# Attention in residue-class order, with 512-token MLP groups interleaved with the next batch's attention

## The chip, the cores and the metric

One core of one Trainium2 chip. The metric is the device time of one execution in microseconds (us); each kernel has three or four executions in rounds shared with the kernel before. Engines: PE is TensorE, PEld its weight loads, DVE VectorE, ACT ScalarE, POOL GpSimd, SP the queue that stores the output. In the kernels, PSUM tiles take what TensorE writes (matmul results and transposes) and SBUF tiles hold everything else; AV is the product of the attention weights with v. The granted clock is the share of its full clock that TensorE was given, as the profile records it.

## The reference, cut to what matters

```python
# q, k, v: (8 batches, 8 heads, 576 tokens, 64), drawn at 0.1 * randn
rel = pos[:, None] - pos[None, :]
mask_plain = (rel >= 0) & (rel < 32)                              # heads 0..3
mask_dil = (rel >= 0) & (rel < 32 * 4) & (rel % 4 == 0)           # heads 4..7
attn = softmax(where(mask, q @ k.T / 8, -1e9)) @ v
x = attn.transpose(0, 2, 1, 3).reshape(4608, 512)
h = x @ w_in                                                       # 512 -> 2048
out = (h * sigmoid(h)) @ w_out                                     # 2048 -> 512
```

Dilated heads look at every fourth token. If tokens are sorted by residue modulo 4 (their class), a dilated head becomes a dense band of 32 within each class of 144 tokens.

## The kernel before

Per batch: transposes of q and k, then five steps over 128-token blocks with scores, exp, mask, AV, and between them the second MLP layer of the batch before; then the whole first MLP layer with nothing beside it.

```python
for nat_t, tT in ((k_nat, kT), (q_nat, qT)):          # 40 transposes, 8 copies of 128x576
    for hp in range(HP):
        tps = ps.tile([P, NC * P], F16, tag="ps", ...)
        for c in range(NC): nc.tensor.transpose(tps[...], nat_t[:ns, c, 2*hp : 2*hp+2, :], ident[...])
        nc.vector.tensor_copy(tT[:, hp, :], tps[:, :S])
# ... cut
for step in range(NC + 2):
    for h in range(H):                                 # scores: keys of a block x 256 queries
        nc.tensor.matmul(sp[:nkv, :nq], kT[...], qT[...], start=True, stop=True)
        nc.scalar.activation(pt[:nkv, :nq], sp[:nkv, :nq], AF.Exp, scale=scale)
        meng = nc.vector if h < 4 else nc.gpsimd       # mask
        meng.tensor_tensor(pt[:nkv, :nq], pt[:nkv, :nq], masks[...], ALU.mult)
    if b > 0 and step < NC: moe_l2(b - 1, step)        # 16 matmuls of 512 columns
    # ... cut: AV, normalisation, transposes back into xT
for f in range(NFF):                                   # first layer: 384 + 192 columns
    for (w0, wn) in L1W:
        for mc in range(4): nc.tensor.matmul(hps[:, :wn], w_in16[...], xT[:, mc, w0:w0+wn], ...)
        nc.scalar.activation(sig[:, :wn], hps[:, :wn], AF.Sigmoid)
        nc.vector.tensor_tensor(gt[:, w0:w0+wn], hps[:, :wn], sig[:, :wn], ALU.mult)
```

The softmax here doesn't subtract the row's maximum and nothing guards it: scores larger than these inputs give would overflow.

## Time and profile before

| | before |
|---|---|
| time | 453.8 us (452.43 to 455.7, 3 runs); 454.27 with the run beside the changed kernel |
| first MLP matmul | 54.3 us |
| period of a batch | 51.1 us: 32.1 attention and second layer, 19.0 first layer |

The page of the kernel before: busy time of each engine, then its PE and PE clock rows (40 equal slices of the span, in tenths), then the chain of waits by engine.

```profile
PE 405.1 (89%) x3041; PEld 240.8 (53%) x3041; DVE 269.2 (59%) x851; ACT 194.2 (43%) x592; POOL 195.0 (43%) x294
...
PE   2670599899999999999999999999999999999996
...
PEclk9999999898999989998999989998999989998999
...
PE 74%; DVE 10%; DMA 5%; POOL 5%; ACT 3%; issue 1%; ACTq 0%; POOLq 0%
```

PE is busy nearly throughout and the chain runs through it, but a busy matmul unit need not be doing much. The windows view divides one period (and looks once more at the first 3.7 us of its first-layer part). Columns: stretch and length, busy us of each engine with the number of instructions, granted TensorE clock, DMA share, GB/s.

```profile
178.70:210.80 32.10, 30.43 (x235) 16.09 (x235) 19.63 (x67) 10.41 (x41) 20.59 (x31) 1.00 0.69 75
210.80:229.80 19.00, 19.00 (x149) 13.54 (x148) 14.28 (x41) 13.83 (x34) 3.45 (x5) 0.91 0.49 33
210.70:214.40 3.70, 3.70 (x19) 2.37 (x18) 1.28 (x9) 2.26 (x4) 3.55 (x5) 0.54 1.11 73
```

The third line is the one to see: at the start of the first layer the clock is about half. The timeline shows what came just before. Columns: start, duration, engine, line, operation, tiles, rows*columns of the weights, output.

```profile
206.88 0.19 PE L195 MATMUL av_3_1_2979<-v_3_1971,p_2_7_2733 128*128 128x65 f16 x1
206.91 0.19 PE L195 MATMUL av_3_1_2979<-v_3_1971,p_3_7_2848 128*128 128x65 f16 x1
...
207.26 0.22 PE L195 MATMUL av_4_0_3003<-v_3_1971,p_3_0_2813 128*64 128x65 f16 x1
207.41 0.21 PE L195 MATMUL av_4_0_3003<-v_3_1971,p_4_0_2909 64*64 64x65 f16 x1
```

AV matmuls with weights of equal size start 0.03 us apart; where the weights alternate between 128 and 64 rows (the last, short block) they start 0.15 us apart. These weights also have fewer columns, but the transposes of q show the same 0.15 us with 128 columns throughout: 0.06 us apart among four of 128 rows, 0.15 us to the one of 64 rows (178.98 to 179.13 us) and again back. The costliest groups of the page add the ScalarE table loads and the wait of the opening: the last column is the idle time before the group and what ended it.

```profile
L241 ACT ACT_TABLE_LOAD x8 | 10.3, 1283 | 61.6 <-PE h_0_0_1406 L233 9.0
L195 PE MATMUL av_3_1_510<-v_0_110,p_3_4_404 128*128 128x65 f16 x1 | 0.2, 233 | 16.9 <-POOL p_3_4_404 L179 16.9
...
L177 ACT ACT_TABLE_LOAD x8 | 10.3, 1283 | 0.9 <-PEq L260 0.8
```

### The profile page before, as it was taken

The page shows a single profiled execution, that of the slowest core. Times are in us where ns is not written, and L with a number is a line of the kernel's source. Part 1 is how long each engine was busy: PE and PEld are TensorE (multiplying, and loading weights), DVE is VectorE, ACT ScalarE, POOL GpSimd, SP SyncE. Part 2 cuts the span into 40 slices and gives each one's busy share as a digit, 9 for nine tenths or more (in the row PEclk, how much of TensorE's full clock was granted, in tenths as well). Part 3 has the DMA queues.
Part 4 walks back from the last instruction along what each step waited for, and adds up shares of the span by engine and source line. Part 5 has one row for each costly group of instructions (what it writes and reads, how often), then busy time and mean ns, then how long its engine had stood idle before and what let it go on. Part 6 is the DMA issues. An engine that isn't in the chain of part 4 may idle for free.

```text
span 454.1 us, 8510 instructions
## 1 busy us (share of the span) xinstructions
PE 405.1 (89%) x3041; PEld 240.8 (53%) x3041; DVE 269.2 (59%) x851; ACT 194.2 (43%) x592; POOL 195.0 (43%) x294
## 2 busy tenths in 40 slices
PE   2670599899999999999999999999999999999996
PEld 1340376346754566446754566446754566446742
DVE  1570277954876468654877468444864468444831
ACT  1450065422764166522764166522764166522710
POOL 9992999953078132953078130540025100540000
PEclk9999999898999989998999989998999989998999
DMA  9999999947197180916296180110001100110011
GB/s 67 153 205 179 103 142 144 135 69 54 12 72 103 37 54 6 145 49 52 15 73 101 36 55 0 48 48 12 2 17 54 37 3 0 48 48 12 3 46 60
DMA packets 120396, 28.35 MB, mean 62 GB/s; under 512 B 113184, under 2 KB 115232, under 8 KB 120352
## 3 DMA queue, kind: packets, MB, share of 16 engines
q0 software_dynamic: 115104, 18.36, 55.6%
q1 hardware_dynamic: 5248, 9.44, 6.0%
q8 instruction: 24, 0.39, 0.4%
q14 instruction: 20, 0.16, 0.1%
HBM read 36.70 MB, written 9.44 MB: 102 GB/s over the span
## 4 chain that ended last, share of the span: by engine, by line
PE 74%; DVE 10%; DMA 5%; POOL 5%; ACT 3%; issue 1%; ACTq 0%; POOLq 0%
DMA w_out_129<-in_moe_w_out_dram 5%; PE o_2_1090 L114 1%; POOL q_nat_108 L94 1%; POOL v_1_365 L101 1%; POOL v_0_110 L101 1%; POOL k_nat_109 L94 1%; PE o_1_5952 L114 1%; PE o_1_5129 L114 1%; PE o_1_4306 L114 1%; PE o_1_3483 L114 1%; PE o_1_2660 L114 1%; PE o_1_1837 L114 1%; PE o_2_4382 L114 1%; PE o_2_3559 L114 1%; PE o_2_6028 L114 1%
## 5 line engine op out<-in xcount | busy, mean ns | idle before, releaser
L233 PEld LDWEIGHTS <-w_in_127 128*128 128x128 f16 x1024 | 98.7, 104 | 39.9 <-issue 9.0
L241 ACT ACT_TABLE_LOAD x8 | 10.3, 1283 | 61.6 <-PE h_0_0_1406 L233 9.0
L195 PE MATMUL av_3_1_510<-v_0_110,p_3_4_404 128*128 128x65 f16 x1 | 0.2, 233 | 16.9 <-POOL p_3_4_404 L179 16.9
L179 POOL TENSOR_TENSOR p_0_4_5874<-p_0_4_5874,masks 128x256 f16<-128x256 f16 x1 | 0.7, 668 | 29.6 <-ACT p_0_4_5874 L177 29.6
L179 POOL TENSOR_TENSOR p_0_4_5051<-p_0_4_5051,masks 128x256 f16<-128x256 f16 x1 | 0.7, 669 | 29.6 <-ACT p_0_4_5051 L177 29.6
L203 DVE RECIPROCAL rcp_3_1_519<-av_3_1_510 128x4 f32<-128x4 f32 x1 | 0.2, 182 | 19.5 <-PE av_3_1_510 L195 19.5
L94 POOL DMA_DIRECT2D q_nat_3615<-in_q_dram x5 | 4.3, 859 | 16.1 <-PE tps_3_1700 L149 16.1
L94 POOL DMA_DIRECT2D q_nat_5261<-in_q_dram x5 | 4.3, 861 | 16.0 <-PE tps_3_3346 L149 16.0
L94 POOL DMA_DIRECT2D q_nat_4438<-in_q_dram x5 | 4.3, 855 | 16.1 <-PE tps_3_2523 L149 16.1
L177 ACT ACT_TABLE_LOAD x8 | 10.3, 1283 | 0.9 <-PEq L260 0.8
L241 ACT ACTIVATE sig_0_0_588<-h_0_0_583 128x384 f16<-128x384 f32 x1 | 0.5, 490 | 23.6 <-PE h_0_0_583 L233 23.6
L195 PEld LDWEIGHTS <-p_3_4_404 128*128 128x128 f16 (+1 forms) x2 | 0.2, 115 | 17.1 <-POOL p_3_4_404 L179 17.0
L179 POOL TENSOR_TENSOR p_0_4_4228<-p_0_4_4228,masks 128x256 f16<-128x256 f16 x1 | 0.7, 665 | 19.3 <-ACT p_0_4_4228 L177 19.3
L94 POOL DMA_DIRECT2D k_nat_364<-in_k_dram x5 | 4.3, 862 | 8.4 <-DMA w_out_129<-in_moe_w_out_dram 8.4
L154 DVE COPY qT_131<-tps_0_161 128x576 f16<-128x576 f16 x1 | 0.5, 457 | 12.1 <-PE tps_1_168 L149 12.1
L149 PE MATMUL tps_0_133<-ident,k_nat_109 128*128 128x128 f16 (+1 forms) x5 | 1.4, 276 | 6.6 <-DMA k_nat_109<-in_k_dram 6.6
L177 ACT ACTIVATE p_0_0_193<-s_0_0_191 128x256 f16<-128x256 f32 x1 | 0.4, 383 | 15.2 <-PE s_0_0_191 L168 15.2
L101 POOL DMA_DIRECT2D v_6_4440<-in_v_dram x5 | 4.3, 881 | 6.0 <-PE xps_3_2_3033 L215 6.0
L101 POOL DMA_DIRECT2D v_7_5263<-in_v_dram x5 | 4.3, 882 | 6.0 <-PE xps_3_2_3856 L215 6.0
L101 POOL DMA_DIRECT2D v_5_3617<-in_v_dram x5 | 4.3, 878 | 6.0 <-PE xps_3_2_2210 L215 6.0
L101 POOL DMA_DIRECT2D v_4_2794<-in_v_dram x5 | 4.3, 871 | 6.0 <-PE xps_3_2_1387 L215 6.0
L168 PEld LDWEIGHTS <-kT_132 64*128 64x128 f16 (+1 forms) x40 | 2.6, 111 | 6.1 <-DVE out_sb_189 L204 1.8
(4102 smaller groups left out, 1587.6 us busy)
## 6 DMA issues: line engine op xcount, KB each, us to landing
w_in_127<-in_moe_w_in_dram POOLq DMA_DIRECT2D x1, 2048.0 KB, 15.2
w_out_129<-in_moe_w_out_dram POOLq DMA_DIRECT2D x1, 2048.0 KB, 24.6
q_nat_108<-in_q_dram POOLq DMA_DIRECT2D x4, 128.0 KB, 4.0
k_nat_109<-in_k_dram POOLq DMA_DIRECT2D x4, 128.0 KB, 4.3
v_0_110<-in_v_dram POOLq DMA_DIRECT2D x4, 128.0 KB, 4.3
q_nat_363<-in_q_dram POOLq DMA_DIRECT2D x4, 128.0 KB, 15.8
k_nat_364<-in_k_dram POOLq DMA_DIRECT2D x4, 128.0 KB, 15.4
v_1_365<-in_v_dram POOLq DMA_DIRECT2D x4, 128.0 KB, 6.6
```

The costliest lines, as they stand in the source:

```text
L94: nc.gpsimd.dma_start(out=dst[:ns, c], in_=src[b, :, src_sl, :].rearrange("h p d -> p h d"),)
L101: nc.gpsimd.dma_start(out=v16[:ns, :, c, :D], in_=v[b, :, src_sl, :].rearrange("h p d -> p h d"),)
L114: nc.tensor.matmul(ops_[:ntk], gts_b[f][:, tb * P : tb * P + ntk], w_out16[:, f, :], start=(f == 0), stop=(f == NFF - 1),)
L149: nc.tensor.transpose(tps[:, c * P : c * P + ns], nat_t[:ns, c, 2 * hp : 2 * hp + 2, :], ident[:ns, :ns],)
L154: nc.vector.tensor_copy(tT[:, hp, :], tps[:, :S])
L168: nc.tensor.matmul(sp[:nkv, :nq], kT[hi * D : hi * D + D, hp, c * P : c * P + nkv], qT[hi * D : hi * D + D, hp, c * P : c * P + nq], start ...
L177: nc.scalar.activation(pt[:nkv, :nq], sp[:nkv, :nq], AF.Exp, scale=scale)
L179: meng.tensor_tensor(pt[:nkv, :nq], pt[:nkv, :nq], masks[:nkv, headtype(h), :nq], ALU.mult)
L195: nc.tensor.matmul(av[:nqt, j, :65], probs[h][cc][r0 : nkv_of[cc], qoff : qoff + nqt], v16[r0 : nkv_of[cc], h, cc, :65], start=(si == 0), ...
L203: nc.vector.reciprocal(rcp[:nqt], av[:nqt, :, 64:65])
L233: nc.tensor.matmul(hps[:, :wn], w_in16[:, mc, f * P : f * P + P], xT[:, mc, w0 : w0 + wn], start=(mc == 0), stop=(mc == DM // P - 1),)
L241: nc.scalar.activation(sig[:, :wn], hps[:, :wn], AF.Sigmoid)
```

## The change: intent and diff

Tokens are kept in class order from the load to the output: the q and k loads fetch four tokens (1 KB) at a time, dilated heads use dense 72-query blocks, plain heads 96-query blocks. The MLP runs over the flattened 4608 tokens in nine groups of 512. The next batch's attention is cut into 38 units that are dealt out over the 32 steps of a group in a fixed order. The diff replaces nearly the whole body; its core, cut. Here and below the diffs are shortened: some lines are joined or reworded, with the same effect.

```diff
-    sig: nc.scalar.activation(sig[:, :wn], hps[:, :wn], AF.Sigmoid); vector multiply
+    nc.scalar.activation(th, h, AF.Tanh, scale=0.5)           # 128x512
+    nc.vector.scalar_tensor_tensor(gT[:, f], th, 1.0, h, ALU.add, ALU.mult)   # the missing factor 0.5 comes with the output copy
-    meng = nc.vector if h < 4 else nc.gpsimd
+    nc.vector.tensor_tensor(pm, pm, mk, ALU.mult)             # two heads, 128x576
-    ps = ctx.enter_context(tc.tile_pool(name="ps", bufs=8, space=PSUM))
+    ps_mm, bufs=3;  ps_s (scores), bufs=1;  ps_a (AV), bufs=2;  ps_t (transposes), bufs=1
+        qP = qkt.tile([P, HP // 2, DIL, M], F16, ...)         # plain heads, class-major
+        kP = qkt.tile([P, HP // 2, M, DIL], F16, ...)         # plain heads, token order
+        def trans(nm, hp):                                    # 8 transposes of 72 tokens, then
+            if hp >= HP // 2: one vector copy of 128x576      #   dilated heads
+            for hi in range(2):                               #   plain heads: four copies
+                for ri in range(2):
+                    if nm == "k":
+                        dst = kP[hs, hp].rearrange("p m (a i) -> p i a m", i=2)[:, ri]
+                    else:
+                        dst = qP[hs, hp].rearrange("p (a i) m -> p i a m", i=2)[:, ri]
+                    nc.scalar.copy(dst, src[rs, hi])          # 64x288
+    for g in range(NG):                                       # nine groups of 512 tokens
+        att = attention(g + 1) if g + 1 < B else []
+        for i, step in enumerate(mlp(g)):                     # 16 first-layer, 16 second-layer
+            step()
+            # ... then the units of att that are due
```

The units of `att` begin with `trans k 0, trans q 0, trans k 1, scores 0, trans q 1`. `kP`: its innermost step m moves by four elements, that of `qP` by one. The keys of a score matmul are its weights; token order in `kP` lets it read 128 neighbouring tokens as one run.

## The prediction

> What bounds the kernel now. The page gives PE 89% of 454.1 us, and the chain of waits is 74% PE. The instruction timeline shows 54.3 us before the first MLP matmul, then a period of 51.1 us per batch, then 39 us for the last one's MLP and tail. The windows view splits a period into 32.1 us (attention with the previous batch's second MLP layer) and 19.0 us (first layer alone, nothing beside it). The second layer streams 80 matmuls of 512 columns, 216 ns apart (timeline): 17.3 us, one fifth of them for a half-empty 64-token block. So about 15 us of a period is attention on PE, of which I count only 7 us of streaming (transposes 56 ns apart, AV 30 ns). The AV of the last block, whose weights alternate 128 and 64 rows, runs at 146 ns. After that thin stretch the first 3.7 us of the first layer get a granted clock of 0.54 (windows), costing 1.7 us per batch. This agrees with the Trainium skill, "TensorE: Matmul & The Clock Gate", section "HAM oscillation". At the start, GpSimd masks queue behind loads: PE waits 16.9 us for a mask.
>
> What changes.
> 1. The MLP becomes 9 groups of exactly 512 tokens: 128 matmuls of 512 columns each, 27.6 us per group, 248 us in all (before: 262 us at full clock).
> 2. Attention per batch goes from 172 matmuls to 204 shorter ones; from the pitches above I estimate 6.5 us of PE. Scores on ScalarE fall from 40 exps (about 10 us) to 8 of 576 columns (about 0.55 us each, estimated from 0.85 ns per column).
> 3. All masks go to VectorE; GpSimd only issues loads, with q/k in 1 KB runs.
> 4. Sigmoid becomes tanh: the built program has one table load, where the trace has 16 of 1.28 us. The skill, "ScalarE: Activation LUTs", section "Table sets", lists exp and tanh in one set.
> 5. Attention of the next batch is dealt out between MLP steps, so PE should keep its clock.
>
> Where PE will still wait. One PSUM buffer serves all transposes and one serves scores. In the first four steps of a group each transpose unit is emptied by four ScalarE copies (about 0.3 us each), queued behind a tanh (about 0.5 us): a step of about 1.75 us against 1.1 us of PE. Walking the queues with these durations gives about 21 us for the first-layer half (18 of PE work) and 17.5 to 18 us for the second. So about 39 us per group, against a PE floor of 34. ScalarE about 20 us, VectorE about 26 us busy per group, not binding on average.
>
> The time. Start: the first batch's attention has nothing to overlap with; q/k land at about 7 to 10 us, then a serial chain through one transpose and one score buffer: first MLP matmul at about 38 us (before 54). Then 8 x 39 = 312, last group 28, tail 3: 381 us.
>
> Chances: faster by over 2% 0.97, within 2% 0.02, slower 0.01. Range 363 to 399.
>
> What would show it: group period 37 to 41 us; clock 0.97 or more during first-layer stretches; PE waiting for ScalarE copies at the q and k transposes; nothing on table loads; POOL only issuing DMA; first MLP matmul at 35 to 42 us.
>
> What would make it wrong: late loads (second batch's q/k or the output weights queued behind 4 MB of input weights) stalling the first group; switches between 64-row score matmuls and 128-row ones costing PE more than 0.15 us; VectorE slowed by GpSimd's load issuing, as one mask multiply before took 3.4 us against 0.29; or the transposes' stalls cutting the clock again, which would push a group to 43 us.

## The result

| | before | changed |
|---|---|---|
| time, median of 4 | 454.27 us | 419.35 us (418.24 to 419.85) |
| first MLP matmul | 54.3 us | 40.1 us |
| steady period | 51.1 us per batch | 45.5 us per group with attention, 27.6 us without |

The ratio is 0.923 (95% interval 0.918 to 0.928). Ratios here are the mean time of one kernel's fast runs over that of the other's of the same rounds, so not quite the ratio of the medians. The kernel became faster by 7.7%, against 16% predicted: 419 lies outside the range of 363 to 399. Of the 36 us between the two profiled spans, 14 come from the opening (54.3 to 40.1 us) and 22 from the rest.

The page after (the same rows as before):

```profile
PE 351.6 (84%) x2784; PEld 175.1 (42%) x2784; DVE 221.0 (53%) x578; ACT 218.8 (52%) x373; POOL 85.2 (20%) x128
...
PE   0266699978996799969997899779995999999996
...
PEclk9999989986999699988998699969997799999999
...
PE 68%; ACT 16%; DVE 11%; issue 3%; DMA 1%; POOL 0%; ACTq 0%; DVEq 0%; POOLq 0%
```

ScalarE's share of the chain went from 3% to 16%, and PE and its clock dip once per group. The windows of one group, cut where the fifth first-layer step and the first layer end:

```profile
86.08:99.76 13.68, 9.81 (x65) 4.36 (x64) 3.12 (x5) 12.77 (x23) 0.00 (x0) 0.65 0.07 20
99.76:113.22 13.46, 13.15 (x126) 6.51 (x125) 11.63 (x24) 9.82 (x17) 6.26 (x8) 0.97 0.50 56
113.22:131.12 17.90, 17.06 (x149) 8.82 (x147) 11.17 (x40) 3.04 (x5) 2.96 (x4) 1.00 0.92 112
```

The second half (17.9 us) is as predicted, and steps 6 to 16 (13.5 us) are close to it. The first five steps take 13.7 us where the walk through the queues had about 8 (four steps of 1.75 us and one of 1.1). Over six steady groups, the second to the seventh, the first-layer half takes 27.5 us on average, where the prediction has 21. ScalarE is busy for 12.8 of them and the clock is 0.65. Its timeline in that stretch:

```profile
87.14 0.60 ACT L311 ACTIVATE th_0_1141<-h_0_1136 128x512 f32<-128x512 f32 x1 [0.22 <-PE h_0_1136 L303]
87.64 3.19 ACT L182 COPY kP_1132<-tk_0_1144 64x288 f16<-64x288 f16 x4
90.85 0.60 ACT L311 ACTIVATE th_1_1162<-h_1_1157 128x512 f32<-128x512 f32 x1
91.55 1.60 ACT L182 COPY qP_1131<-tq_0_1165 64x288 f16<-64x288 f16 x4
93.25 0.60 ACT L311 ACTIVATE th_2_1183<-h_2_1178 128x512 f32<-128x512 f32 x1
93.88 3.20 ACT L182 COPY kP_1132<-tk_1_1186 64x288 f16<-64x288 f16 x4
```

Gaps of 0.1 us at most: ScalarE works from one item to the next. Four k copies take 3.2 us, four q copies of the same shape, from the same PSUM buffer and with the same partition shift, 1.6 us. PE's side of it, the longest wait of the group:

```profile
90.87 0.22 PE L164 MATMUL tq_0_1165<-ident,q_nat_0_547 72*128 72x72 f16 x1 [2.64 <-ACT kP_1132 L182]
```

The other lines of before have these counterparts: AV no longer alternates weight sizes, so its matmuls start 0.03 us apart, and one table load is left.

```profile
120.25 0.19 PE L234 MATMUL av_d_1539<-vd_105,probs_99 128*128 128x65 f16 x1
120.28 0.20 PE L234 MATMUL av_d_1539<-vd_105,probs_100 128*128 128x65 f16 x1
```

```profile
L182 ACT ACT_TABLE_LOAD x1 | 1.3, 1283 | 0.8 <-PEq L378 0.8
```

### The profile page after: what moved, and what is told of

It is laid out like the page before. It is cut to its first block, busy times and chain, and to the rows that moved or that the text cites. A ratio compares the mean times of both kernels' runs of the same rounds, so it can differ in the third digit from the quotient of the medians.

```text
span 417.9 us, 7058 instructions
## 1 busy us (share of the span) xinstructions
PE 351.6 (84%) x2784; PEld 175.1 (42%) x2784; DVE 221.0 (53%) x578; ACT 218.8 (52%) x373; POOL 85.2 (20%) x128
## 4 chain that ended last, share of the span: by engine, by line
PE 68%; ACT 16%; DVE 11%; issue 3%; DMA 1%; POOL 0%; ACTq 0%; DVEq 0%; POOLq 0%
ACT kP_192 L182 2%; DMA k_nat_1_113<-in_k_dram 1%; ACT kP_2292 L182 1%; ACT kP_2873 L182 1%; ACT kP_1132 L182 1%; ACT kP_4025 L182 1%; ACT kP_3452 L182 1%; ACT kP_1713 L182 1%; ACT kP_552 L182 1%; PE y_0_1454 L321 1%; PE y_0_3195 L321 1%; PE y_0_2035 L321 1%; PE y_0_874 L321 1%; PE y_0_4347 L321 1%; PE y_0_3774 L321 1%
## 5 line engine op out<-in xcount | busy, mean ns | idle before, releaser
L303 PEld LDWEIGHTS <-w_in_88 128*128 128x128 f16 x576 | 53.4, 106 | 56.5 <-issue 14.9
L100 POOL DMA_DIRECT2D vp_104<-in_v_dram x24 | 18.0, 751 | 23.6 <-DMA w_in_88<-in_moe_w_in_dram 5.3
L100 POOL DMA_DIRECT2D vp_103<-in_v_dram x24 | 17.9, 754 | 18.2 <-DMA q_nat_0_1708<-in_q_dram 2.4
L224 DVE TENSOR_TENSOR probs_91<-probs_91,mask_p 128x576 f16<-128x576 f16 x3 | 1.4, 454 | 15.3 <-ACT probs_91 L222 15.3
L321 PEld LDWEIGHTS <-gT_4800 128*128 128x128 f16 x64 | 6.3, 98 | 7.5
L321 PEld LDWEIGHTS <-gT_4587 128*128 128x128 f16 x64 | 6.2, 97 | 7.6
L82 POOL DMA_DIRECT2D k_nat_0_2283<-in_k_dram x1 | 0.8, 848 | 31.0 <-PE tk_3_1897 L164 31.0
L82 POOL DMA_DIRECT2D k_nat_0_3443<-in_k_dram x1 | 0.8, 848 | 30.5 <-PE tk_3_3057 L164 30.5
L82 POOL DMA_DIRECT2D k_nat_0_2864<-in_k_dram x1 | 0.8, 848 | 30.3 <-PE tk_3_2476 L164 30.3
L321 PEld LDWEIGHTS <-gT_555 128*128 128x128 f16 x64 | 5.3, 97 | 4.1
L321 PEld LDWEIGHTS <-gT_3455 128*128 128x128 f16 x64 | 5.3, 97 | 4.1
L321 PEld LDWEIGHTS <-gT_2876 128*128 128x128 f16 x64 | 5.3, 97 | 4.1
L321 PEld LDWEIGHTS <-gT_4028 128*128 128x128 f16 x64 | 5.3, 97 | 4.1
L321 PEld LDWEIGHTS <-gT_2295 128*128 128x128 f16 x64 | 5.3, 97 | 4.1
L321 PEld LDWEIGHTS <-gT_1716 128*128 128x128 f16 x64 | 5.3, 97 | 4.1
L321 PEld LDWEIGHTS <-gT_1135 128*128 128x128 f16 x64 | 5.3, 97 | 4.1
L182 ACT COPY kP_192<-tk_0_195 64x288 f16<-64x288 f16 x4 | 3.2, 790 | 7.1 <-PE tk_0_195 L164 7.1
L94 POOL DMA_DIRECT2D vraw_107<-in_v_dram x8 | 5.9, 744 | 4.2 <-DMA w_out_89<-in_moe_w_out_dram 3.1
L311 ACT ACTIVATE th_0_561<-h_0_556 128x512 f32<-128x512 f32 x1 | 0.6, 597 | 11.5 <-PE h_0_556 L303 11.5
L94 POOL DMA_DIRECT2D vraw_108<-in_v_dram x8 | 5.9, 743 | 3.1 <-DMA w_in_88<-in_moe_w_in_dram 1.7
L82 POOL DMA_DIRECT2D k_nat_0_1704<-in_k_dram x1 | 0.8, 848 | 27.0 <-PE tk_3_1316 L164 27.0
```

What stands on the lines that cost most here:

```text
L82: nc.gpsimd.dma_start(out=d.rearrange("p h r d -> p h (r d)"), in_=src[b].rearrange("h (m r) d -> m h (r d)", r=DIL)[t * MH : (t + 1) * MH],)
L94: nc.gpsimd.dma_start(out=vraw[p0 : p0 + n, ab].rearrange("p h r d -> p h (r d)"), in_=src[m0 : m0 + n],)
L100: nc.gpsimd.dma_start(out=vp[:, j, :, :D], in_=v[b, :HN, k0 : k0 + P, :].rearrange("h p d -> p h d"),)
L182: nc.scalar.copy(dst, src[rs, hi])
L224: nc.vector.tensor_tensor(pm, pm, mk, ALU.mult)
L303: nc.tensor.matmul(h, w_in16[:, c, f * P : (f + 1) * P], xT[:, c, t0 : t0 + GT], start=(c == 0), stop=(c == HP - 1),)
```

## The experiments

Three theories. A: ScalarE is the limit of the first five steps, and the k copies, which write every fourth element, are what overloads it. B: the single transpose buffer is the limit, whatever the copies write. C: the halved clock is the cost. In the tables, "five steps" is the time from the first matmul of a group's first step to that of its sixth, in one steady group; "group" is the steady period.

The five steps are a cut that work can cross: units that a stretch doesn't finish are paid for in the steps after it. So where buffers or engines are changed (experiments 3, 6 and 7), read the first-layer half too.

### 1. k copies without a step (wrong)

```diff
-        kP = qkt.tile([P, HP // 2, M, DIL], ...)
+        kP = qkt.tile([P, HP // 2, DIL, M], ...)
-        dst = kP[hs, hp].rearrange("p m (a i) -> p i a m", i=2)[:, ri]
+        dst = kP[hs, hp].rearrange("p (a i) m -> p i a m", i=2)[:, ri]
-        kP[r, hp].rearrange("p m r -> p (m r)")[:, k0 : k0 + P]
+        kP[r, hp].rearrange("p r m -> p (r m)")[:, k0 : k0 + P]   # other keys
```

> Wrong result on purpose: kP is stored class-major, so the ScalarE copies of the k transposes write runs of 144 elements as those of q do, and the score matmuls read the same number of weights, of other keys. Theory A (the first-layer half of a group is bound by ScalarE, whose k copies take 0.79 us because they write every fourth element, against 0.39 us for q): the k copies fall to 0.39 us, the first five steps of a group from 13.7 to about 10.5 us, 7 groups x 3.2 us plus 3.2 us in the opening attention: about 394 us. Theory B (the one transpose buffer and the order of the steps stall PE, whatever a copy writes): copies may get shorter, but the time stays within 2% of 419. Theory C (the halved TensorE clock of that stretch is the cost): under 10 us gained unless the clock there rises from 0.65 to above 0.9.

Measured: 386.12 us, ratio to before 0.853 (0.850 to 0.856). Groups of instructions, columns as above:

```profile
L180 ACT COPY kP<-tk 64x288 f16<-64x288 f16 x64 | 25.1, 392 | 9.4 <-PE tk L164 8.4
L180 ACT COPY qP<-tq 64x288 f16<-64x288 f16 x64 | 25.1, 392 | 2.4 <-PE tq L164 1.8
```

The k copies now cost what the q copies cost, five steps take 8.9 us in two groups (9.7 to 9.8 us in the four after them) and a group 40.8 us. B's claim that the time stays is refuted. The gain of 33 us is larger than the 25 expected. One warning: the comparison with the reference passed, although the plain heads read other keys than they should. Inputs of 0.1 make all scores nearly zero and all weights nearly equal, so the comparison says little about which keys are read. That the other variants are right follows from their access patterns.

### 2. The dose the other way: q copies with the step

```diff
-        qP = qkt.tile([P, HP // 2, DIL, M], ...);  dst: "p (a i) m -> p i a m"
+        qP = qkt.tile([P, HP // 2, M, DIL], ...);  dst: "p m (a i) -> p i a m"
-        qP[r, hp, :, QM * j : QM * (j + 1)]
+        qP[r, hp].rearrange("p m r -> p r m")[:, :, QM * j : QM * (j + 1)]
```

> The dose the other way: qP is stored like kP, so the q copies also write every fourth element. Right result. Theory A: q copies go from 0.39 to about 0.79 us, the first five steps grow by 3.2 us per group, 7 x 3.2 + 3.2 = about +25 us: about 444 us. Theory B: no change in time beyond 2%. If the score matmuls' moving operand is slow to read with that stride, PE score groups would get longer than 0.30 us as well.

Measured: 439.25 us, ratio 0.970 (0.967 to 0.974), 20 us more than the changed kernel; the group grew by 2.2 us to 47.6.

```profile
L182 ACT COPY qP<-tq 64x288 f16<-64x288 f16 x64 | 50.6, 791 | 1.8 <-PE tq L164 0.7
```

The q copies doubled as expected. Together the two runs fix the cause of the slow copies to the step of the destination, since shape, source and engine stayed. The 20 us are not all due to the copies. The five steps grew by 1.4 to 1.8 us, not by 3.2 (the first-layer half by 2.2 us), and the score matmuls became slower too, which the expectation had named as a possibility: with q read four elements apart, six of them take 0.36 us until the next matmul starts instead of 0.23 at full clock. Over the 32 such groups of a kernel that is up to 3.9 us (an estimate from these two durations).

### 3. k copies on VectorE

```diff
-                    nc.scalar.copy(dst, src[rs, hi])
+                    (nc.vector.tensor_copy if nm == "k" else nc.scalar.copy)(dst, src[rs, hi])
```

> The layout is left as it is; the k copies go to VectorE, which was busy 3.1 of the 13.7 us of the first five steps. Right result. Theory A (ScalarE is the engine that binds the stretch): ScalarE loses 6.4 us there; if VectorE writes that stride without a penalty (about 0.35 us a copy, estimated from its 0.45 us for 576 elements of the other transposes), the stretch falls to 8 to 9 us and the kernel to about 380 us; if VectorE doubles too (0.7 us), to about 395 us. Theory B (one transpose buffer): the gain stays below 8 us, as the next transpose still waits for the copies. Theory C: the clock of the stretch rises with the gain.

Measured: 434.43 us, ratio 0.961 (0.956 to 0.966): slower than the changed kernel by 15 us, where 380 to 395 was expected. A miss, and an instructive one.

```profile
L183 DVE COPY kP<-tk 64x288 f16<-64x288 f16 x64 | 50.6, 791 | 8.8 <-PE tk L164 8.2
```

VectorE takes 791 ns for the same copy, to the nanosecond what ScalarE took for q in experiment 2. The windows view of one such stretch:

```profile
227.10:242.00 14.90, 9.55 (x63) 4.09 (x63) 9.28 (x13) 6.68 (x15) 0.00 (x0) 0.65 0.06 18
```

With ScalarE relieved (busy 6.7 of 14.9 us), the five steps still took 14.0 us in one group and 15.2 in another. So theory A as stated, ScalarE alone, is wrong: a second limit of nearly the same length lies right behind it. Why the kernel became slower than the changed one, and not only no faster, is not shown.

### 4. TensorE kept busy in its waits

```diff
             step()
+            fill = {1: 22, 2: 8, 3: 20, 4: 12}.get(i, 0) if att else 0
+            if fill:
+                junk = ps_a.tile([P, HN, 66], F32, tag="a", ...)
+                for n in range(fill):
+                    nc.tensor.matmul(junk.rearrange("p h d -> p (h d)"), ident,
+                                     w_in16[:, 0, : HN * 66], start=True, stop=True)
```

> 62 matmuls of 264 columns on constants, whose result nobody reads, are put into the waits of steps 1 to 4 of each group with attention, so that TensorE stays busy and its clock is not cut. Right result. Theory C (the cut clock costs the time): granted clock of the first five steps from 0.65 to above 0.9, and 10 us or more gained. Theory A: the clock rises likewise, but ScalarE is the limit of the stretch, so the time changes by less than 2% (between 411 and 427 us).

Measured: 414.46 us, ratio 0.916 (0.913 to 0.920). The five steps of a group in the windows view:

```profile
86.34:99.90 13.56, 13.38 (x128) 9.30 (x127) 3.12 (x5) 12.86 (x23) 0.00 (x0) 1.00 0.07 21
```

The clock is at full speed over the whole execution (mean 1.000 against 0.931), and five steps still take 13.5 us. The group settles at 44.5 us against a mean of 45.5 (it varied between 44.6 and 46.3 without the filling). So the halved clock is worth about 3 to 5 us of the kernel (3 by the ratios, 5 by the medians and the profiled spans); C is refuted as the main cause. The two kernels' intervals against before overlap slightly, so the size is rough; the steady period shows it better.

### 5. The disputed cost by itself

Copies appended at the end of the changed kernel, four per engine and pattern, one engine at a time:

```diff
+    for _ in range(4): nc.scalar.copy(scrA[:64, : 288 * S].rearrange("p (n s) -> p n s", s=S)[:, :, 0],
+                                      tm[:64, :288])                    # S = 1, 2, 4, 8, 16
+    for _ in range(4): nc.vector.tensor_copy(... the same into scrV ...)
+    # and runs of 2, 4, 8 elements with equal gaps
```

> The changed kernel, with PSUM-to-SBUF copies of 64x288 two-byte elements appended at its end, four on ScalarE and four on VectorE for each destination pattern: steps of 1, 2, 4, 8, 16 elements, and runs of 2, 4 and 8 elements with equal gaps. Theory S (a write port serves runs: single two-byte elements that stand apart pay, whatever the engine): about 0.39 us at step 1 and about 0.79 us at steps 2 to 16 on ScalarE, with runs of 4 (8 bytes) back at 0.39. Theory L [...]: steps 1, 2 and 4 at 0.39, 8 and 16 slower; but then the kernel's own step of 4 would not have cost 0.79, so something else in it would be the cause (the split into two source rows, or the partition shift). The time itself says nothing (about 20 us longer).

Columns: count, minimum/median/maximum in ns, first and last start. In this order: step 1 on ScalarE and VectorE, step 2 on ScalarE, step 4 on both, step 8 and step 16 on ScalarE, runs of 2 with a gap of 2 on both, runs of 2 with a gap of 6 on both.

```profile
L370 ACT COPY scrA<-tm x4: 380/392/392, 412.9 to 414.2; 64x288 f16<-64x288 f16 x4
L371 DVE COPY scrV<-tm x4: 298/299/299, 414.6 to 415.6; 64x288 f16<-64x288 f16 x4
L372 ACT COPY scrA<-tm x4: 472/472/472, 416.0 to 417.5; 64x288 f16<-64x288 f16 x4
...
L374 ACT COPY scrA<-tm x4: 788/788/788, 420.1 to 422.5; 64x288 f16<-64x288 f16 x4
L375 DVE COPY scrV<-tm x4: 785/786/787, 423.3 to 425.8; 64x288 f16<-64x288 f16 x4
L376 ACT COPY scrA<-tm x4: 1422/1423/1424, 426.7 to 431.0; 64x288 f16<-64x288 f16 x4
...
L378 ACT COPY scrA<-tm x4: 1352/1352/1353, 438.4 to 442.5; 64x288 f16<-64x288 f16 x4
...
L380 ACT COPY scrA<-tm x4: 392/392/392, 449.5 to 450.8; 64x288 f16<-64x288 f16 x4
L381 DVE COPY scrV<-tm x4: 299/300/301, 451.2 to 452.2; 64x288 f16<-64x288 f16 x4
...
L386 ACT COPY scrA<-tm x4: 404/404/405, 458.8 to 460.1; 64x288 f16<-64x288 f16 x4
L387 DVE COPY scrV<-tm x4: 401/402/402, 460.5 to 461.8; 64x288 f16<-64x288 f16 x4
```

Both expected shapes were wrong: the cost is neither all or nothing at step 2 nor absent until step 8. It rises with the step (on ScalarE 0.47, 0.79 and 1.42 us at steps 2, 4 and 8, about 0.16 us for each element of step; on VectorE the same within 2 ns) and stays at about 1.4 us for a step of 16. Runs of two adjacent elements with a gap of two cost nothing on either engine; with a gap of six they take 0.40 us, a third more than without gaps on VectorE. A step of 4 gives 0.79 us on both engines without the split into two source rows and without a partition shift, so those are cleared; a copy over 128 partitions with step 4 took 0.795 us too.

Theory L is what the Trainium skill, "SBUF — State Buffer", section "Door 1: The DMA port swizzle", leads to expect: it speaks of 16-byte lines, of at least two accesses per line for full bandwidth, and of steps of up to 8 bf16 elements as free. A step of 4 two-byte elements has two per line and still doubles the copy (0.788 against 0.392 us), so the measurement does not agree. "Vector Engine (DVE) Microarchitecture Reference", section "5.2 Measured stream behaviour on trn2", says that for the full rate consecutive elements must come in runs of at least two adjacent 4-byte words; it measured 4-byte elements in SBUF. That runs matter agrees with the sweep. For the two-byte elements here a run of a single 4-byte word (two elements) was enough with a gap of one word (0.300 against 0.299 us on VectorE), not with a gap of three (0.402 us).

### 6. A second transpose buffer

```diff
-    ps_a = tc.tile_pool(name="ps_a", bufs=2, ...);  ps_t = tc.tile_pool(name="ps_t", bufs=1, ...)
+    ps_a = tc.tile_pool(name="ps_a", bufs=1, ...);  ps_t = tc.tile_pool(name="ps_t", bufs=2, ...)
```

> A second transpose buffer, paid for with one of the two AV buffers. Right result. Theory A (ScalarE is the limit of the first five steps): that stretch stays at 13 to 13.7 us, because ScalarE still has 12.7 us of work in it; the second half may get up to 2.5 us longer per group by the AV buffer; time 410 to 437 us. Theory B (the single transpose buffer): the stretch falls by 3 us or more.

Measured: 438.59 us, ratio 0.965 (0.962 to 0.969); five steps 12.2 us, group 47.8 us. The stretch fell by 1.5 us, short of B's 3, with ScalarE busy for 11.5 of its 12.2 us. Even this gain was only moved: the first-layer half took 27.6 us (27.5 before the edit), as the steps after the fifth became longer. The missing AV buffer lengthened the second half from 17.9 to 20.2 us (PE waits of 0.73 us at each of the four pairs of dilated AVs), so the time landed 2 us above the expected range.

### 7. Both: k copies on VectorE and a second transpose buffer

> The same second transpose buffer under the variant whose k copies are on VectorE (434 us). If that variant lost because k and q copies, now on two engines, still went one after the other through one buffer (3.2 + 1.6 + 3.2 + 1.6 us plus hand-overs), then two buffers let them overlap and the stretch of about 15 us falls to about 9 to 11 us, 4 to 6 us per group, less up to 2.5 us for the AV buffer: 405 to 425 us. If it lost because VectorE was too slow for its other work, the stretch stays at 14 us or more.

The edits of 3 and 6 together. Measured: 410.24 us, ratio 0.904 (0.900 to 0.907); five steps 7.5 us, group 43.3 to 45.1 us. Against experiment 3 one buffer more took the stretch from between 14.0 and 15.2 us to 7.5 us, although the slow copies were all still there; 1.8 us of that reappear in steps 6 to 8, among them a PE wait of 1.5 us for k copies. The first-layer half, mean of six steady groups in us, counts both:

| | k copies on ScalarE | k copies on VectorE |
|---|---|---|
| one transpose buffer | 27.5 (changed kernel) | 29.2 (experiment 3) |
| two transpose buffers | 27.6 (experiment 6) | 24.0 (experiment 7) |

The second half is 17.9 us in the upper row and 20.2 us in the lower one, which has one AV buffer less.

This separates the limits: with one buffer the copies of k and q must follow each other (3.2 + 1.6 + 3.2 + 1.6 us, plus transposes, hand-overs and the work queued before them); on one engine they must follow each other as well, with five tanhs. Lifting either alone leaves 12 to 15 us for the five steps and no gain in the half. Slow copies lengthen both, which is why only shortening them (experiment 1) helped by itself.

### 8. Plain heads in token order (right result)

Without the class-order load for the plain heads no copy needs a step, and one transpose fills 128 partitions with two heads:

```diff
+            d = natp.tile([P, NC, HN, D], F16, tag="natp", ...)        # plain heads, token order
+            for c in range(NC):
+                nc.gpsimd.dma_start(out=d[:n, c], in_=src[b, :HN, c*P : c*P+n, :].rearrange("h p d -> p h d"))
-                d = nat.tile([MH, H, DIL, D], ...)                     # all heads, class order
+                d = nat.tile([MH, HN, DIL, D], ...)                    # dilated heads only
+            if hp < HP // 2:                                           # in trans()
+                for c in range(NC): nc.tensor.transpose(tpl[...], nats[nm, "pl"][:n, c, 2*hp : 2*hp+2, :], ident[:n, :n])
+                nc.scalar.copy((kP if nm == "k" else qP)[:, hp], tpl[:, :S])      # 128x576
-        kP[r, hp].rearrange("p m r -> p (m r)")[:, k0 : k0 + P],  qP[r, hp, :, QM * j : QM * (j + 1)]
+        kP[r, hp, k0 : k0 + P],  qP[r, hp, QB * j : QB * (j + 1)].rearrange("p (m r) -> p r m", r=DIL)
```

> A candidate for the best version, right result: k and q of the plain heads are loaded in token order (as the kernel before did), so one 128x576 copy empties a transpose of two heads, without a stride; the score matmuls read q with a stride of four instead. Theory A: ScalarE's copies fall from 9.6 to about 2.1 us per group (4 x 0.53), the first five steps from 13.7 to 7 to 8 us, the group from 45.4 to about 38.5 us, the opening attention by about 6 us: about 363 us (355 to 372), with the clock near 1. Rival: the 20 extra small loads per batch delay the first groups and give back 5 us or more.

Measured: 371.13 us, ratio 0.818 (0.814 to 0.822): faster than both kernels. One copy of 0.63 to 0.64 us stands where four stood; five steps take 7.1 us, a group 38.3 us, and the clock is 0.998.

```profile
L182 ACT COPY kP<-tk 128x576 f16<-128x576 f16 x16 | 10.1, 634 | 12.1 <-PE tk L177 12.1
L182 ACT COPY qP<-tq 128x576 f16<-128x576 f16 x16 | 10.2, 640 | 1.5 <-PE tq L177 1.5
```

The group is as expected, although its score matmuls read q with a step and take 0.36 us a group of six, as in experiment 2. The total is 8 us above the expected 363: the opening gained 3.3 us, not 6, and the first group took 43.2 us. The rival, more small loads, is only partly borne out. (It counts 20 extra loads per batch; the edit adds ten.) TensorE first waited until 12.1 us for the identity, which GpSimd made after issuing 14 loads. But in the first group PE's waits for loads add up to 1.5 us of the 5; its first two MLP steps also ran at half pace (1.9 us each instead of 1.0).

### 9. The same with its loads reordered

```diff
-    issue_qk(0)
     make_identity(nc, ident)
+    issue_qk(0)
...
     for f0 in range(0, DFF, FC):
         nc.gpsimd.dma_start(out=w_in16[:, :, f0 : f0 + FC], ...)
-    issue_qk(1)
+        if f0 == 0: issue_qk(1)
```

> The token-order version (371 us) with its start mended, right result: the identity is made before the loads, and the second batch's q and k are issued after the first quarter of the input weights instead of after all four. In the version before, TensorE waited until 12.1 us for the identity, and the first group took about 43 us against 38.3 for the later ones. If the order of the loads was the reason, the first transpose starts at about 8 us (4 us gained) and the first group falls by 2 to 5 us: about 364 us. If the loads' bandwidth is the limit instead, the first group gives back what the start gains: 368 us or more.

Measured: 372.79 us, ratio 0.818 (0.813 to 0.824): no gain. The first transpose started at 4.3 us instead of 12.1, but PE then waited for loads one after the other, the first MLP matmul came at 36.2 us (36.8 before), and the output weights came late in the first group (one wait of 2.5 us). So the wait moved from the identity to the loads; whether another order or larger loads would shorten the first 80 us stays open.

## Why the prediction was wrong, point by point

The sum of the prediction beside what the trace shows:

| term | predicted | measured |
|---|---|---|
| first MLP matmul | 38 | 40.1 |
| groups with attention | 8 x 39 = 312 | 7 x 45.5 = 318.3 |
| groups without attention | 28 | 2 x 27.6 = 55.3 |
| tail | 3 | 4.3 |
| sum (span) | 381 | 417.9 |

- **The step that failed** is "each transpose unit is emptied by four ScalarE copies (about 0.3 us each)", and with it "about 21 us for the first-layer half", which took 27.5 us. The k copies took 0.79 us and the q copies 0.39 us, so ScalarE had 9.6 us of copies per group instead of 4.8. The prediction does not say where its 0.3 us comes from, and it nowhere mentions the destination's step, which stood in the diff. Experiments 1, 2 and 5 show that the step of four elements is what makes the k copies slow. The mechanism, copies queued behind a tanh, was right: with the measured durations (copies of 0.79 and 0.39 us, a tanh of 0.60) the prediction's own walk gives about 13.0 us for the five steps (an estimate), and 13.7 were measured.
- **The size of it.** Groups with attention took 6.5 us longer than predicted, 45 us over seven. Copying k without the step returns 4.5 us per group, 32 us, part of it through the clock; the remaining 2.0 us per group are about what 16 copies at 0.40 instead of 0.30 us add (1.6 us, worked out, not tested alone).
- **An error that hid part of this.** Eight groups were counted with attention. The first batch's attention runs in the opening and there are seven more, so two groups are bare. With the count right, the prediction's own numbers give 38 + 273 + 56 + 3 = 370 us, further off.
- **Right in kind**: PE waits for ScalarE copies at the q and k transposes, as named. But "ScalarE" was only half of it: the single buffer, which the prediction also named, is a second limit of nearly equal length (experiments 3, 6 and 7).
- **The clock.** Predicted was 0.97 or more in first-layer stretches; it was 0.65 in the first five steps, as the prediction's last warning had it. Its own cost is small, about 3 to 5 us (experiment 4), because the matmuls were waiting anyway. The Trainium skill, "TensorE: Matmul & The Clock Gate", section "HAM oscillation", tells of a clock cut by waits longer than about 3.4 us. The trace agrees that waits cut the clock (0.65 there, 1.00 when they were filled), but not on the length: the longest wait here was 2.64 us, and in the kernel before, no wait above 0.25 us preceded the 0.54 at the start of the first layer.
- **Right**: 40.1 us to the first MLP matmul (35 to 42 said), 17.9 us for the second half (17.5 to 18), 27.6 us for a bare group, GpSimd only issuing loads after the opening, and one table load left, as the skill's "ScalarE: Activation LUTs", section "Table sets", led one to expect. The fear of switches between 64-row score matmuls and 128-row ones did not come true: at full clock the six score matmuls of two plain heads took 0.23 us of PE, and the next MLP step began right after them. Nor did the fear of slowed masks: all 64 took 0.45 to 0.46 us. (The 3.4 us mask that the prediction cites ran mostly beside four masks of GpSimd; the three after it, beside load issues, took 0.95 to 0.96 us.)

## What to carry to other kernels

Before costing a PSUM-to-SBUF copy by its column count, read the destination's innermost step: single two-byte elements four apart took a copy to 0.79 us, from 0.39 on ScalarE and from 0.30 on VectorE, so moving it to another engine was no cure; a layout that writes runs was. A step moved to the matmul's reading side is not free either (0.36 against 0.23 us for six score matmuls), but here it was the cheaper place. When two resources (here an engine and a single buffer) serialise the same chain, freeing either one alone shows little, and the experiment that frees both, or shortens the work itself, tells the truth. Count the stages that have overlap and those that have none before multiplying.

## What the Trainium skill lacked or had wrong

- "SBUF — State Buffer": by its 16-byte lines ("Door 1: The DMA port swizzle"), two-byte elements four or eight apart should be free; they cost 0.79 and 1.42 us against 0.39 for 64x288 (ScalarE). No page gives this cost for ScalarE writes.
- "Vector Engine (DVE) Microarchitecture Reference", section 5.2: it has no figure for two-byte elements. Runs of one 4-byte word (two elements) ran at full rate with a gap of one word, 0.300 against 0.299 us, and took 0.402 us with a gap of three.
- "ScalarE: Activation LUTs", section "What ACT_TABLE_LOAD costs": it lets back-to-back ACTIVATEs overlap by about 93 ns, and here they overlapped by 0.10 us. It has no figure for COPY instructions, which did not overlap: four of 0.39 us took 1.60 us.
- "TensorE: Matmul & The Clock Gate": alternating weights of 128 and 64 rows made small matmuls start 0.15 us apart instead of 0.03; it has no number for it. Nor does a page have one for a moving operand read with a step: six score matmuls with q four elements apart took 0.36 us instead of 0.23.
